# Conversion pieces moved into the expert slots, the first relu on ScalarE, the next tokens turned later

## The chip, the cores and the metric

One core of one Trainium2 chip runs the whole program. The metric is the device time of one execution in microseconds, as the median of several runs; a lower time is better.

## The reference

The program chains three layers on 1792 tokens of width 768. What matters here is the middle one, a layer of 8 experts, each token going to the one expert with the largest gate value:

```python
attn = 1.0 / (1.0 + np.exp(-scores));  x = attn @ v            # 4 x 12 heads, 448 x 64
e_idx = np.argmax(x @ w_gate, axis=1)
for e in range(8):                                             # w1[e]: 768 x 1024, w2[e]: 1024 x 768
    h = np.maximum(x[e_idx == e] @ w1[e], 0.0)
    out[e_idx == e] = gate_w * eom * (h @ w2[e])
h = out @ w_in;  return (h * np.cos(h)) @ w_out                # w_in: 768 x 2048, w_out: 2048 x 768
```

The weights `w_in` and `w_out` of the last layer arrive as 64-bit floats, the others as 32-bit floats.

## The kernel before

**Numbers.** A matrix product is made of three matmuls: each 32-bit operand is split into a high part (rounded by ScalarE, `hi`) and a low part (the rest, by VectorE, `lo`), and high x high, high x low and low x high are added up in PSUM. The helper `split` does this for raw expert weights (L217 on ScalarE, L218 on VectorE).

**Stages.** Attention takes the first 240 us or so, the experts go on to about 598 us, and the last layer follows.

**Slots.** After the tokens have been sorted by expert, the expert stage works in slots of 128 tokens: `slot(s, ...)` (L737) for s = 0, 1, 2 and so on. An expert has one slot or more; a slot either goes on with the expert of the slot before or begins a new one. Which slots are new, and which are used at all, is known only at run time: flags in `fl` are read into registers, and `tc.If(new != 0)` guards what a new expert needs. Slots 0 to 13 are always used (`NSURE` is 14), later ones are under a branch of their own. In this execution slots 0 to 18 are used, and 4, 6, 10, 11, 14, 15 and 18 begin an expert.

**One slot on TensorE.** The first product has two halves of 512 columns, each with 6 steps of 3 matmuls (`mm1`). Each half goes through a relu (`hr0`, `hr1`), is turned by 4 transposes and split (`turn_h`: `hh` on ScalarE, `hl` on VectorE). The second product has 8 steps of 6 matmuls (`mm2`), the first four of which use the first half. The next slot's tokens, gathered by GpSimd, are turned by 6 transposes and split into `xh` and `xl` (`turn`, L228). At the end `scale_y` scales the result, and SP stores it.

**The order.** The schedule is manual: every engine's queue holds its instructions in the order in which the program issues them. In a slot with s > 1 VectorE's order is: relu `hr0`; low part of the second weights 0 (`split2(0)`); `hl` of the first half; low part 1; relu `hr1`; `xl` (two operations); low parts 2 and 3; `hl` of the second half; the four low parts of the next expert's first weights (`split1(s + 1)`); the scaling; a conversion piece. ScalarE has the high parts at the same places. The low and high parts of weights are there only in slots that begin an expert, or stand before one.

**Weight loads.** The raw weights of an expert pass through four buffers `rw`. When `split1` has split a quarter of the first weights, SP loads a quarter of the second weights into the same buffer (L735); when `split2(i)` has split that, SP loads a quarter of the following expert's first weights (L757).

**Conversion pieces.** The 64-bit weights of the last layer are brought into high and low parts in 48 pieces. `conv(i)` is a generator with a first part (ScalarE two operations, GpSimd a maximum, VectorE two operations, L154 to L158) and, after a `yield`, a second part (VectorE four operations, L160 to L163). `conv_step` ends a begun piece, lets SP store the finished one and load the piece after this one, and begins the next; with `whole` it runs both parts at once. 23 pieces are converted during attention; before the change slots 1 to 17 do one whole piece each at their end, as the last lines of `slot` say, and the last 8 come in the last stage.

Of the kernel before, what the change touches and what calls it, by code (L numbers as in the profile page):

```python
# [22 lines left out]

GATE_STEPS = 7
NEST = 18
CONV_EARLY = 40
PAUSE = "pause"
NRING = 6
ROUTE_AT = [(0, "relu"), (0, 9), (0, 13), (0, 15), (1, 0), (1, 3), (1, "relu"), (1, 9), (1, 14)]
# [25 lines left out]
def tile_attn_moe_cos(ctx: ExitStack, tc: tile.TileContext, q, k, v, wg, wog, w1, w2, w_in, w_out, out):  # L55
# [13 lines left out]
    NSURE = -(-NT // P)  # L69
# [60 lines left out]
    def conv_load(i):  # L130
        if i >= len(conv_list):
            return
        which, h, r = conv_list[i]
        raw = craw[i % 2]
        if which == "i":
            src = w_in[r * P : (r + 1) * P, h * CW : (h + 1) * CW].bitcast(U32)
            nc.sync.dma_start(raw.rearrange("p f t -> p (f t)"), src)
        else:
            src = wo_in[h][:, :, r * CO : (r + 1) * CO].bitcast(U32)
            nc.sync.dma_start(raw.rearrange("p (two f) t -> p two (f t)", two=2), src)  # L140
# [25 lines left out]
    def conv_store():  # L166
        while conv_out:
            which, h, r, parts_ = conv_out.pop()
            for t, f in enumerate(parts_):
                if which == "i":  # L170
                    c0 = h * CW // P
                    nc.sync.dma_start(
                        wi_d[c0 : c0 + CW // P, :, t, r, :].rearrange("c p f -> p c f"),
                        f.rearrange("p (c f) -> p c f", f=P),
                    )
                else:
                    nc.sync.dma_start(
                        wo_to[h, t][:, :, r * CO : (r + 1) * CO], f.rearrange("p (two f) -> p two f", two=2)
                    )

    conv_at = [0]

    def conv_step(whole=True):
        conv_end()
        conv_store()
        conv_load(conv_at[0] + 1)
        conv_rest.append(conv(conv_at[0]))
        next(conv_rest[0], None)
        conv_at[0] += 1
        if whole:  # L190
            conv_end()
# [3 lines left out]
    def conv_end():  # L195
        while conv_rest:
            next(conv_rest.pop(), None)
# [9 lines left out]
    def w1_src_d(e, i):  # L207
        nh, kg = divmod(i, 2)
        return w1[bass.ds(e, 1)].rearrange("o (k p) f -> p (o k) f", p=P)[
            :, 3 * kg : 3 * kg + 3, 512 * nh : 512 * nh + 512  # L210
        ]
# [4 lines left out]
    def split(raw, hi, lo, pool):  # L216
        nc.scalar.activation(hi, raw, AF.Copy)  # L217
        (nc.gpsimd if pool else nc.vector).tensor_tensor(lo, raw, hi.bitcast(F32), op=ALU.subtract)  # L218

    def gather(xg, at, rows=NT):  # L220
        nc.gpsimd.indirect_dma_start(
            out=xg,
            out_offset=None,
            in_=x_d[:rows, :],
            in_offset=bass.IndirectOffsetOnAxis(ap=at, axis=0),
        )

    def turn(xg, ps, tag):  # L228
        for k0, n_ in ((0, 4), (4, 2)):
            pt = ps.tile([P, 512], F32, tag=tag, name="pxt")  # L230
            for kc in range(n_):
                nc.tensor.transpose(pt[:, kc * P : (kc + 1) * P], xg[:, (k0 + kc) * P : (k0 + kc + 1) * P], ident)
            ptv = pt[:, : n_ * P].rearrange("p (k t) -> p k t", t=P)
            nc.scalar.activation(xh[:, k0 : k0 + n_], ptv, AF.Copy)  # L234
            nc.vector.tensor_tensor(
                xl[:, k0 : k0 + n_], ptv, xh[:, k0 : k0 + n_].bitcast(F32), op=ALU.subtract
            )

    def mm1(ps, nh, kc, first, last):
        i = 2 * nh + kc // 3  # L240
        wh, wl = w1h[i][:, kc % 3, :], w1l[i][:, kc % 3, :]
        nc.tensor.matmul(ps, xh[:, kc], wh, start=first, stop=False)  # L242
        nc.tensor.matmul(ps, xh[:, kc], wl, start=False, stop=False)  # L243
        nc.tensor.matmul(ps, xl[:, kc], wh, start=False, stop=last)  # L244


    with ExitStack() as st:
# [314 lines left out]
        for i in range(n):  # L562
# [8 lines left out]
            elif 6 <= i < 6 + NSLOT - NSURE:  # L571
                s = NSURE + i - 6
# [109 lines left out]
    with ExitStack() as st:  # L682
        wp = st.enter_context(tc.tile_pool(name="wp", bufs=1, reuse_waits="tile"))
        m2 = st.enter_context(tc.tile_pool(name="m2", bufs=2, reuse_waits="tile"))
        ps_t = st.enter_context(tc.tile_pool(name="ps_t", bufs=4, reuse_waits="tile", space=PSUM))
# [6 lines left out]
        xgs = [xg0] + [wp.tile([P, DM], F32, name="xg1")]  # L692
        ysbs = [wp.tile([P, ROW], F32, name=f"ysb{i}") for i in range(3)]

        def relu(ps, scalar=False):
            hr = m2.tile([P, 512], F32, tag="hr", name="hr")
            if scalar:
                nc.scalar.activation(hr, ps, AF.Relu)
            else:
                nc.vector.tensor_scalar(hr, ps, 0.0, None, op0=ALU.max)  # L700
            return hr
# [22 lines left out]
        def flag(row, s, engines, top=1):  # L724
            return nc.values_load(fl[0:1, row, s : s + 1], engines=engines, min_val=0, max_val=top)
# [11 lines left out]
        def slot(s, between, when):  # L737
            nxt = s + 1 < NSLOT
            ahead = min(s, 1)
            hh = m2.tile([P, KF, P], F32R, tag="hh", name="hh", bufs=1)  # L740
            hl = m2.tile([P, KF, P], F32R, tag="hl", name="hl", bufs=1)
            with when():
                if 0 < s < NSLOT - 2:
                    gather(xgs[s % 2], idx[:, s + 2 : s + 3])
                if s > 1:
                    new = flag(1, s, SPLIT)
                    ld = flag(3, s, [ENG.SP])
                    ne = flag(0, s, [ENG.SP], E - 1)

                def split2(i):  # L750
                    if s == 0:
                        split(w2r[i], w2h[i], w2l[i], i in (0, 2))
                    elif s > 1:
                        with tc.If(new != 0):
                            split(w2r[i], w2h[i], w2l[i], False)
                        with tc.If(ld != 0):
                            nc.sync.dma_start(w1r[i], w1_src_d(ne, i))  # L757

                ph = p0 if s == 0 else ps_h.tile([P, 512], F32, tag="h", name="p0")
                for kc in range(3 if s == 0 else 0, KD):  # L760
                    mm1(ph, 0, kc, kc == 0, kc == KD - 1)
                    between(kc)
                hr0 = relu(ph)
                between("relu")
                split2(0)
                p1 = ps_h.tile([P, 512], F32, tag="h", name="p1")
                for kc in range(KD):
                    mm1(p1, 1, kc, kc == 0, kc == KD - 1)
                    if kc == 2:
                        turn_h(hr0, hh, hl, 0)  # L770
                        split2(1)
                    between(KD + kc)
                hr1 = relu(p1, s <= 1)
                if 0 < s and nxt:
                    turn(xgs[(s + 1) % 2], ps_t, "t")
                if s > 0:
                    split2(2)
                    split2(3)
                py = ps_y.tile([P, 2, 512], F32, tag="y", name="py")
                state["py"] = py  # L780
                for kc in range(ahead):
                    mm2(py, hh, hl, kc)
                    between(2 * KD + kc)
                turn_h(hr1, hh, hl, 1)
                between("h")
                if s == 0:
                    split2(2)
                    split2(3)
            if nxt and s >= NSURE:
                split1(s + 1)  # L790
            with when():
                for kc in range(ahead, KF):
                    mm2(py, hh, hl, kc)
                    between(2 * KD + kc)
                if s == 0:
                    turn(xgs[1], ps_t, "t")
                elif nxt and s < NSURE:
                    split1(s + 1)
                if s > 0:
                    scale_y(s)  # L800
            if s >= 1 and conv_at[0] < CONV_EARLY:
                conv_step()

        def scale_y(s):
# [7 lines left out]
        def store_y(s):  # L812
            nc.sync.dma_start(ys_d[s * P : (s + 1) * P, :], ysbs[s % 3])
# [191 lines left out]
        def between(s):  # L1005
            def step(k):
                for _ in range(ROUTE_AT.count((s, k))):
                    next(route, None)

            return step  # L1010
# [2 lines left out]
            split(w1r[i], w1h[i], w1l[i], pool)  # L1013
            nc.sync.dma_start(w2r[i], w2_src_d(e1[0], i))
        def last_slots(s):
            assert conv_at[0] >= CONV_EARLY
            act = nc.values_load(fl[0:1, 2, s : s + 1], min_val=0, max_val=1)
            with tc.If(act != 0):
                slot(s, between(s), nullcontext)
                store_y(s)  # L1020
                if s + 1 < NSLOT:
                    last_slots(s + 1)
# [22 lines left out]
    with ExitStack() as st:  # L1045
# [178 lines left out]
        for u in range(N):  # L1224
# [3 lines left out]
            turn = ()  # L1228
            if bi + 1 < len(blocks):
                if 1 <= c < 5:  # L1230
                    gather_y(bi + 1, c - 1)
                if 8 <= c < 8 + KD:
                    turn = turn_y(bi + 1, c - 8)
# [43 lines left out]
```

## Time and profile before

| | us |
|---|---|
| median of 3 runs | 1092.7 |
| lowest and highest of them | 1090.5, 1092.93 |
| the profiled execution: its time | 1094.78 |
| its span in the profile | 1093.0 |
| TensorE matmul busy in it | 1040.6 (95%) |
| VectorE busy | 703.8 (64%) |
| ScalarE busy | 486.1 (44%) |

The profile is of one execution. Its span runs from the first instruction to the last; the execution's own time is a little longer. PE is TensorE (PEld its weight loads), DVE is VectorE, ACT is ScalarE, POOL is GpSimd, SP issues most DMAs. Matmuls are pipelined, so that the recorded time of one is longer than the distance to the next. Times in the timeline count from the start of the span.

### The profile page before, as it was taken

The page shows a single profiled execution, that of the slowest core. Times are in us where ns is not written, and L with a number is a line of the kernel's source. Part 1 is how long each engine was busy: PE and PEld are TensorE (multiplying, and loading weights), DVE is VectorE, ACT ScalarE, POOL GpSimd, SP SyncE. Part 2 cuts the span into 40 slices and gives each one's busy share as a digit, 9 for nine tenths or more (in the row PEclk, how much of TensorE's full clock was granted, in tenths as well). Part 3 has the DMA queues.
Part 4 walks back from the last instruction along what each step waited for, and adds up shares of the span by engine and source line. Part 5 has one row for each costly group of instructions (what it writes and reads, how often), then busy time and mean ns, then how long its engine had stood idle before and what let it go on. Part 6 is the DMA issues. An engine that isn't in the chain of part 4 may idle for free. (4 is left out here: it accounts for less than half of the span.)

```text
span 1093.0 us, 16911 instructions
## 1 busy us (share of the span) xinstructions
PE 1040.6 (95%) x5836; PEld 832.6 (76%) x5836; DVE 703.8 (64%) x1229; ACT 486.1 (44%) x706; POOL 186.1 (17%) x189
## 2 busy tenths in 40 slices
PE   7999998889999999899798899999999999999997
PEld 4555555468878887687687788788888899999996
DVE  3778778576667458658747589865455555665553
ACT  6777775532435246336334344334323343334332
POOL 4433332521210211210211032103000020001001
PEclk9999999999999999899999999999999999999999
DMA  6999895635488429839845998656744478667741
GB/s 193 269 292 301 248 270 178 229 109 198 143 291 290 145 96 333 301 132 345 275 140 192 350 376 313 246 204 245 253 180 174 176 286 302 258 234 281 258 170 44
DMA packets 118788, 254.68 MB, mean 233 GB/s; under 512 B 9440, under 2 KB 66016, under 8 KB 118688
## 3 DMA queue, kind: packets, MB, share of 16 engines
q1 hardware_dynamic: 114768, 234.19, 63.1%
q0 software_dynamic: 3920, 19.28, 4.7%
q8 instruction: 48, 0.79, 0.3%
q14 instruction: 52, 0.43, 0.1%
HBM read 207.02 MB, written 46.41 MB: 232 GB/s over the span
## 5 line engine op out<-in xcount | busy, mean ns | idle before, releaser
L1169 PE MATMUL o<-wo,gh 128*128 128x512 f32 x448 | 168.4, 397 | 0.0
L155 POOL TENSOR_SCALAR cta<-cta 128x512 f32<-128x512 f32 x48 | 77.4, 1613 | 458.6 <-ACT cta L154 439.0
L1109 PE MATMUL ph<-yh,wi 128*128 128x512 f32 (+1 forms) x318 | 115.3, 363 | 0.2 <-DMA wi<-wi_d 0.2
L1110 PE MATMUL ph<-yl,wi 128*128 128x512 f32 (+1 forms) x318 | 115.2, 362 | 0.0
L1111 PE MATMUL ph<-yh,wi 128*128 128x512 f32 (+1 forms) x318 | 115.1, 362 | 0.0
L301 ACT ACTIVATE aT<-sc,b_sig 112x896 f32<-112x896 f32 x96 | 91.7, 1005 | 49.3 <-PE sc L298 48.1
L1132 ACT ACTIVATE r<-r 128x512 f32<-128x512 f32 (+1 forms) x64 | 37.0, 579 | 168.2 <-DVE r L1127 166.6
L1170 PE MATMUL or<-wo,gh 128*128 128x256 f32 x384 | 108.3, 282 | 0.0
L1169 PEld LDWEIGHTS o<-wo,gh 128*128 128x128 f32 x448 | 84.2, 188 | 17.0
L242 PE MATMUL p<-w1h,xh 128*128 128x512 f32 x228 | 93.2, 409 | 0.5 <-ACT xh L234 0.5
L243 PE MATMUL p<-w1l,xh 128*128 128x512 f32 x228 | 90.9, 398 | 0.5 <-DVE w1l L218 0.5
L244 PE MATMUL p<-w1h,xl 128*128 128x512 f32 x228 | 90.5, 397 | 0.0
L1169 PE MATMUL o<-wo,gl 128*128 128x512 f32 x224 | 88.2, 394 | 0.0
L305 PE MATMUL av<-aT,v 112*64 112x448 f32 x384 | 84.2, 561 | 0.0
L1138 DVE TENSOR_TENSOR r<-r,p 128x512 f32<-128x512 f32 (+1 forms) x64 | 40.0, 626 | 66.4 <-ACT r L1133 66.4
L1193 POOL DMA_INDIRECT out_dram<-osb,at x14 | 14.2, 1017 | 368.3 <-DVE osb L1182 277.0
L1170 PEld LDWEIGHTS or<-wo,gh 128*128 128x128 f32 x384 | 72.3, 188 | 0.8
L1123 DVE TENSOR_SCALAR t<-p 128x512 f32<-128x512 f32 (+1 forms) x64 | 27.2, 425 | 65.7 <-ACT p L1118 65.7
L709 ACT ACTIVATE hh<-pht 128x512 fp32r<-128x512 f32 x38 | 22.8, 599 | 101.4 <-PE pht L706 91.2
L1118 ACT ACTIVATE p<-ph 128x512 f32<-128x512 f32 (+1 forms) x64 | 34.7, 542 | 71.5 <-PE ph L1111 71.5
L1109 PEld LDWEIGHTS ph<-yh,wi 128*128 128x128 f32 x318 | 59.7, 188 | 8.4 <-DMA wi<-wi_d 0.7
L1143 DVE TENSOR_TENSOR gl<-r,gh 128x512 fp32r<-128x512 f32 (+1 forms) x64 | 42.5, 664 | 36.4 <-ACT gh L1142 36.4
(257 smaller groups left out, 2454.1 us busy)
## 6 DMA issues: line engine op xcount, KB each, us to landing
rw<-in_moe_w_dram SPq DMA_DIRECT2D x64, 768.0 KB, 6.5
wo<-wo_d SPq DMA_DIRECT2D x64, 768.0 KB, 4.5
wi<-wi_d SPq DMA_DIRECT2D x53, 768.0 KB, 6.0
craw<-in_moe_w_in_dram SPq DMA_DIRECT2D x25, 512.0 KB, 6.3
craw<-in_moe_w_out_dram SPq DMA_DIRECT2D x24, 512.0 KB, 5.3
er<-wi_d SPq DMA_DIRECT2D x11, 768.0 KB, 6.1
ys_d<-ysb SPq DMA_DIRECT2D x19, 384.5 KB, 3.6
wi_d<-chi SPq DMA_DIRECT2D x24, 256.0 KB, 3.8
```

Source lines behind the costliest of these rows:

```text
L155: nc.gpsimd.tensor_scalar(ta.bitcast(F32), ta.bitcast(F32), LEAST, None, op0=ALU.max)
L242: nc.tensor.matmul(ps, xh[:, kc], wh, start=first, stop=False)
L243: nc.tensor.matmul(ps, xh[:, kc], wl, start=False, stop=False)
L244: nc.tensor.matmul(ps, xl[:, kc], wh, start=False, stop=last)
L301: nc.scalar.activation(aT[:, c], ps[:, :, :S], AF.Sigmoid, bias=b_sig[:CP], scale=1.0 / math.sqrt(D))
L305: nc.tensor.matmul(pav[D * j : D * j + D, :S], t["v"][:, j, c, :], aT[:, c, j], start=c == 0, stop=c == NC - 1)
L1109: nc.tensor.matmul(ph[:, :w], wih[:, kc], yh[:, kc, :w], start=kc == 0, stop=False)
L1110: nc.tensor.matmul(ph[:, :w], wih[:, kc], yl[:, kc, :w], start=False, stop=False)
L1111: nc.tensor.matmul(ph[:, :w], wil[:, kc], yh[:, kc, :w], start=False, stop=kc == KD - 1)
L1143: nc.vector.tensor_tensor(gl[:, :w], r, gh[:, :w].bitcast(F32), op=ALU.subtract)
L1169: nc.tensor.matmul(acc[i], g[:, ts_], w[:, :512], start=f, stop=l)
L1170: nc.tensor.matmul(acc["r", i], g[:, ts_], w[:, 512:], start=f and (own or i % 2 == 0), stop=l, skip_group_check=True,)
```

## The change

- The first relu of a slot (`hr0`) runs on ScalarE instead of VectorE in all slots but slot 0.
- In those slots its transposes come after step 3 of the second half of the first product instead of step 2, and `split2(1)` moves from there behind the second relu.
- `split2(2)` and `split2(3)` come behind the transposes of the second half (`turn_h(hr1, ...)`) instead of ahead of them.
- In slots 1 to 13 the next tokens are turned after step 3 of the second product instead of before its first step; in the later slots they stay where they were, behind `split2(1)` now.
- The 17 conversion pieces of the slots no longer stand at the end of slots 1 to 17. Eight slots (`CONV_1ST`) begin a piece behind the turning of the first half, and end it (`conv_end`) behind the second weights' splits. Six of them (`CONV_2ND`) then begin a second piece, which ends behind the turning of the next tokens. Three slots (`CONV_END`) do a whole piece at their end. "Begin" includes the store of the piece before and the load of the next on SP.

```diff
-CONV_EARLY = 40
+CONV_1ST = (1, 2, 3, 6, 7, 8, 11, 12)
+CONV_2ND = (2, 3, 6, 7, 8, 11)
+CONV_END = (14, 15, 17)
...
-                hr0 = relu(ph)
+                hr0 = relu(ph, s > 0)
...
-                    if kc == 2:
+                    if kc == (3 if s > 0 else 2):
                         turn_h(hr0, hh, hl, 0)
-                        split2(1)
+                        if s == 0:
+                            split2(1)
+                        if s in CONV_1ST:
+                            conv_step(False)
                     between(KD + kc)
                 hr1 = relu(p1, s <= 1)
-                if 0 < s and nxt:
+                if s > 0:
+                    split2(1)
+                if s >= NSURE and nxt:
                     turn(xgs[(s + 1) % 2], ps_t, "t")
-                if s > 0:
-                    split2(2)
-                    split2(3)
...
                 turn_h(hr1, hh, hl, 1)
                 between("h")
-                if s == 0:
-                    split2(2)
-                    split2(3)
+                split2(2)
+                split2(3)
+                conv_end()
+                if s in CONV_2ND:
+                    conv_step(False)
...
                     mm2(py, hh, hl, kc)
                     between(2 * KD + kc)
+                    if kc == 3 and 0 < s < NSURE:
+                        turn(xgs[(s + 1) % 2], ps_t, "t")
+                        conv_end()
...
-            if s >= 1 and conv_at[0] < CONV_EARLY:
+            if s in CONV_END:
                 conv_step()
```

## Rows read from the trace of the kernel before

**Rows 1.** Busy time by slot: start:end, length, busy (count) by engine, clock, DMA.
```profile
277.83:296.05 18.22, 18.22 (x100) 15.46 (x99) 12.57 (x17) 9.48 (x11) 2.83 (x2) 1.00 0.42 135
...
334.51:354.41 19.90, 18.81 (x101) 15.39 (x99) 15.57 (x20) 9.29 (x11) 2.64 (x2) 1.00 1.01 351
354.41:372.75 18.34, 18.33 (x100) 15.45 (x99) 7.69 (x14) 3.88 (x7) 2.82 (x2) 1.00 0.41 133
...
409.39:429.31 19.92, 18.78 (x101) 15.39 (x99) 16.52 (x21) 11.31 (x13) 2.65 (x2) 1.00 1.01 344
429.31:456.83 27.52, 21.62 (x101) 17.48 (x99) 20.33 (x22) 13.21 (x14) 2.95 (x2) 0.88 0.90 312
...
493.27:514.42 21.15, 18.83 (x100) 15.41 (x99) 18.98 (x22) 12.34 (x14) 2.63 (x2) 1.00 0.99 345
514.42:540.28 25.86, 20.06 (x100) 16.57 (x99) 17.77 (x21) 12.04 (x13) 2.95 (x2) 0.93 0.94 315
540.28:559.02 18.74, 18.32 (x100) 15.46 (x99) 7.70 (x14) 3.87 (x7) 2.82 (x2) 1.00 0.70 212
...
577.53:598.20 20.67, 18.69 (x100) 15.27 (x98) 15.95 (x20) 9.29 (x11) 2.87 (x2) 1.00 0.63 219
```

**Rows 2.** Timeline of TensorE, slots 4, 11 and 15: start, length, instruction, [idle before].
```profile
307.74 0.66 PE L706 MATMUL pht<-ident,hr 128*128 128x128 f32 x4 [0.71 <-DVE hr L700]
...
441.05 0.47 PE L706 MATMUL pht<-ident,hr 128*128 128x128 f32 x1 [4.61 <-DVE hr L700]
...
525.71 0.69 PE L706 MATMUL pht<-ident,hr 128*128 128x128 f32 x2 [4.96 <-DVE hr L700]
```

**Rows 3.** Timeline of VectorE in slot 11, up to the first relu.
```profile
434.46 1.76 DVE L218 TENSOR_TENSOR w1l<-rw,w1h 128x1536 fp32r<-128x1536 f32 x1 [0.21 <-ACT w1h L217]
...
437.73 0.47 DVE L160 TENSOR_SCALAR cta<-cta 128x512 uint32<-128x512 uint32 x1
...
440.31 0.69 DVE L700 TENSOR_SCALAR hr<-p 128x512 f32<-128x512 f32 x1 [0.19 <-issue]
```

**Rows 4.** Busy time in slot 11 behind the long wait, columns as in rows 1.
```profile
441.05:445.80 4.75, 4.75 (x13) 3.78 (x14) 3.90 (x3) 1.97 (x2) 0.00 (x0) 0.50 1.04 394
```

**Rows 5.** Timeline of slot 3, all engines.
```profile
279.36 1.63 POOL L155 TENSOR_SCALAR cta<-cta 128x512 f32<-128x512 f32 x1 [15.22 <-ACT cta L154]
279.87 0.78 DVE L158 SCALAR_TENSOR_TENSOR ctu<-ctb,ctu 128x512 f32<-128x512 uint32 x1 [0.23 <-ACTq L754]
...
284.02 0.66 PE L706 MATMUL pht<-ident,hr 128*128 128x128 f32 x4
285.35 0.69 DVE L710 TENSOR_TENSOR hl<-pht,hh 128x512 fp32r<-128x512 f32 x1 [1.38 <-ACTq L754]
286.62 0.82 PE L232 MATMUL pxt<-ident,xg 128*128 128x128 f32 x6
288.32 0.60 PE L706 MATMUL pht<-ident,hr 128*128 128x128 f32 x4
289.55 1.49 ACT L217 ACTIVATE w1h<-rw 128x1536 fp32r<-128x1536 f32 x1
```

**Rows 6.** Groups by line, whole span: count | busy us, mean ns | idle before.
```profile
L217 ACT ACTIVATE w2h<-rw 128x1536 fp32r<-128x1536 f32 x32 | 46.6, 1484 | 5.1 <-DMA rw<-in_moe_w_dram 5.1
L154 ACT ACTIVATE cta<-craw 128x512 f32<-128x512 f32 x48 | 32.0, 668 | 3.3 <-DMA craw<-in_moe_w_in_dram 2.7 <-DMA craw<-in_moe_w_out_dram 0.4
L698 ACT ACTIVATE hr<-p 128x512 f32<-128x512 f32 x2 | 1.2, 598 | 1.5 <-PE p L244 1.4
```

**Rows 7.** DMA issues in slot 6: count, KB each, median us to landing.
```profile
rw<-in_moe_w_dram SPq DMA_DIRECT2D x5, 768.0 KB, 6.8
craw<-in_moe_w_in_dram SPq DMA_DIRECT2D x1, 512.0 KB, 9.8
```

**Rows 8.** Line 735, the loads of second weights.
```profile
DMA to landing us min/median/max: 4.2/6.5/9.1
```

More of the change, by code (lines that the diff above doesn't have):

```diff
@@ L1015, in last_slots @@
         def last_slots(s):
-            assert conv_at[0] >= CONV_EARLY
+            assert s > max(CONV_END)
             act = nc.values_load(fl[0:1, 2, s : s + 1], min_val=0, max_val=1)
```

## Prediction

> **What bounds the kernel now.** I first read the busy time slot by slot, a row for each of the 18 expert slots after the first [rows 1]. In a slot that goes on with an expert TensorE is busy nearly all the time: slots 3, 7 and 16 take 18.22, 18.34 and 18.74 us, and the seven more of their kind that are not shown lie between 18.21 and 18.51 (slot 1, with the routing in it, takes 19.62). A slot that begins an expert shows by its VectorE work (20 operations and more). There are seven: 4, 6, 10, 11, 14, 15 and 18 (4 takes 20.13, much as 10). They hold the idle TensorE time, and 11 and 15, which follow another new expert at once, hold most of it: 9.3 and 7.6 us above slot 3.
>
> Then I read who ended TensorE's waits, in the timeline [rows 2]. The long ones stand before the transposes of a relu's result: 4.61 us in slot 11, 4.96 in slot 15, and 0.71 before the second relu's in slot 4. VectorE's timeline shows why in slot 11 [rows 3]: the last low part of the first weights ends at 436.22, then come the scaling of the slot before and a whole conversion piece (its second half begins at 437.73), and the first relu only at 440.31. The relu is late because it stands in VectorE's order behind the piece. After that wait the granted clock is 0.50, the 1.2 GHz level, for 13 matmuls [rows 4]. The mean clock, 0.88 in slot 11 and 0.93 in slot 15, puts that loss at up to 0.12 x 27.52 = 3.3 and 0.07 x 25.86 = 1.8 us [rows 1].
>
> The change touches what lies between 240 and 598 us. Attention before it and the last stage behind it issue what they did: 23 pieces are converted ahead of the slots and 17 in them, as ever.
>
> **First relu on ScalarE.** It costs 0.60 there [rows 6], and ScalarE is busy 4 to 13 us of a slot [rows 1]. It waits for the product and for what ScalarE has to do before, so the waits of 4.6 and 5.0 go. In slot 15 a piece stays ahead (one of three still put at a slot's end): the scaling and the piece's two ScalarE operations, 0.67 each, leave some 0.6 of wait.
>
> **Pieces inside the slot.** In slots 1, 2, 3, 6, 7, 8, 11 and 12 a piece's first part now stands behind the first half's low part and ahead of the second relu on VectorE (in slot 1 that relu is on ScalarE). Worked from slot 3 [rows 5], in us after its start at 277.83: the transposes of the first relu, at 6.19, come three matmuls later, at 6.9 (27 took the 6.19). Its high part ends 1.33 later, when the low part can begin: 8.2. The piece's first ScalarE operation, 0.67, ends at 8.9; GpSimd's maximum starts then, and VectorE's second operation of the piece ends 1.29 after that start (279.36 to 280.65): 10.2. The relu, 0.69, ends at 10.9. TensorE would be there at 10.49 (288.32) less the six token transposes that moved away, 0.82 with their tail and some 0.7 without: 9.8. So it waits 1.1 in each such slot. The bounds: nothing, if the piece is through before the product is, and 2.2, if the relu also had to wait for most of the maximum. I take 1.1, since each step of it is a row. Slots 2 and 3: +1.1 each, slot 8 +1.0, slot 1 +0.3: **+3.5**.
>
> On this chain the Trainium skill has a rule that speaks against the change (SBUF — State Buffer, section "SBUF: two separate sides"): VectorE with two SBUF inputs and GpSimd reading SBUF lock one pair of ports against each other, and the loser waits for the whole instruction. The trace does not agree: in slot 3 VectorE's operation with two SBUF inputs ran from 279.87 to 280.65, inside the maximum's 279.36 to 280.99 [rows 5]. The sum by that rule is among the rivals; it goes by the row here.
>
> **Second parts and second pieces.** The second half of a piece, 2.4 us of VectorE (437.73 to 440.12 [rows 3]), moves behind the last low parts, where about 7 us of TensorE work follow; that work hides it, and without it the next tokens would be 2.4 late. Slots 2, 3, 6, 7, 8 and 11 start a second piece before the next tokens are turned, and of these 6 and 11 begin an expert. There the second piece's load is issued on SP behind the reload of the first raw weights, which waits for the first low part of the second weights, 8.2 into the slot (relu over at 4.95, then 1.49 [rows 6] and 1.76 [rows 3]); with the two stores before it, it goes out at about 9.5. Even with SP free such a load landed 9.8 after its issue in slot 6, behind weights that took 6.8 [rows 7]. So it lands 19 us into a slot of 19.2. ScalarE's two operations (1.2, overlapped) stand ahead of the next tokens' high part (0.6) and VectorE's ahead of their low part (0.7): with the gaps 2.65 after the landing, 21.7, where TensorE wants it at 19.7. Slot 7 starts 2.0 late, slot 12 by the same count 2.1, and each waits 1.1 for its own piece: 21.3 against 18.34, and 21.4 against 18.2: **+6.2**. Landings of 18 and 19.7 would give 1.0 and 2.7, and behind the weights of slot 11, itself late, up to 5.4 in slot 12: the term lies between +3 and +10.
>
> **New experts.** The next tokens are turned after four steps of the second product, at 13.3 to 14.0. Their high parts end at 14.9, and only then ScalarE splits the next first weights, which it began at 11.7 before (289.55, [rows 5]): some 3.1 later. The first low part is ready at 18.1, just as the slot ends, and the load behind it starts then. In slot 4 a second piece of slot 3 stands before it on VectorE, a wait of 1.8 at the start, which eats the slot's gain (0). Elsewhere the load lands 4.2 after issue [rows 8] and the relu is over at 4.95; with 1.49, 1.76 and the half's low part of 0.69 that is 8.9, wanted by the second product at 9.3: no wait. The second relu no longer stands behind a low part of 1.76, nor the last low part behind two of them, so waits like the 0.71 go. Slot 10: 18.2, -1.7. Slots 14 and 18 keep the token turn ahead, 0.6: 18.8 and 18.7, -2.3 and -2.0. Slot 6 waits 1.1 for its piece: 19.2, -0.7. **-6.7**; bounds -3 (other waits turn up behind those removed) and -8 (none is left).
>
> Slot 11: 18.2, plus 1.5 for the first low part (its loads come at the pace of the DMA, share 1.01 in slot 10), 0.4 for the second weights, 1.6 for the second relu behind low part and piece: 21.7, -5.8. No wait comes near the 4.6 ahead of the half clock, so I count none of that. Slot 15: 18.2 + 0.7 (first low part) + 0.6 (relu) + 2.5 (second weights' low part behind a whole piece on VectorE) + 1.5 (their third low part behind the tokens'): 23.5, -2.4. **-8.2**; bounds -11 and 0, the latter if the landing of the weights sets the pace at each step.
>
> **Slots with no piece before or in them** (5, 9, 13, 16, 17; in 16 it no longer matters) fall to 18.2: **-1.3**, between -1.5 and 0.
>
> **Sum:** 3.5 + 6.2 - 6.7 - 8.2 - 1.3 = -6.5 us. The profiled execution took 1094.78, 1.78 more than its span of 1093.0, and lies 2.1 above the median of 1092.7; against its own time that is 1088.3, against the median **1086.2**.
>
> **Rivals.**
> *Pieces free.* Neither the second relu nor the next tokens wait for a piece: +3.5 and +6.2 go, -16.2 is left, 1076.5. For it: VectorE and ScalarE are far from full in slot 3 [rows 1]. Against: their order is fixed, and the chain above is of recorded steps.
> *Late second pieces.* Their loads land at the upper bound, +10 for +6.2: -2.7, 1090.0, no change by the line below. For it: DMA share 1.01 in slots 6 and 10 [rows 1]. Against: the landing of 9.8 was behind stores and a gather too.
> *Port lock.* VectorE's second operation of the piece starts only at the end of GpSimd's maximum, 280.99 for 279.87, in seven slots: +7.7, so +1.2, 1093.9. Against it: they ran together [rows 5]. This is what the Trainium skill's SBUF — State Buffer says in "SBUF: two separate sides".
> *Late weights, the slower side.* The second weights are asked for 3.1 us later. If their first load lands L after its issue, TensorE waits L - 5.4 (9.3 less 1.49, 1.76 and 0.69) before the second product in slots 4, 6, 10 and 14. The longest landing is 9.1 [rows 8]: 4 x 3.7 = 14.8, so +8.3, 1101. It decides from L = 7.0 on and passes 0.3% slower at 7.9. For it: the median is 6.5. Against: the short landings come when the queue was empty, as it is at the starts of these slots.
>
> **How the numbers follow.** Forecast 0.58, pieces free 0.12, late second pieces 0.16, port lock 0.05, late weights 0.09. 0.3% (3.3 us) is about what a measurement can tell from no change: faster is below 1089.4, slower above 1096. The forecast and pieces free are faster but for 0.04 near the line; of late second pieces 0.02 are faster; port lock is no change; of late weights 0.08 are slower, and 0.03 more of the second pieces, should they meet other upper bounds. That gives 0.68, 0.21 and 0.11. The range 1080 to 1094 holds the forecast with its bounds, late second pieces and port lock, and leaves out most of pieces free and of late weights.
>
> **What would show it.** Right: no wait before the first relu's transposes; clock 1.00 in slot 11; waits near 1.1 before the second relu's in slots 2, 3, 7 and 8; slots 7 and 12 starting 2 us late behind the token turn; slot 11 below 23. Wrong: waits before the second product in slots 6, 10 and 14; a half clock in slot 11 or 15; slots 2 and 8 still at 18.2.

## The result, and the profile after

The changed kernel takes 1106.67 us (median of 4 runs, 1104.88 to 1108.48); the kernel before, run beside it, 1092.82. The ratio is 1.0114, with a 95% interval of 1.0087 to 1.014: slower, where 1086.2 and faster was predicted (range 1080 to 1094). The profiled execution took 1105.22, its span is 1103.5 against 1093.0, and 9.5 of these 10.4 us lie in slots 1 to 18.

The waits of TensorE between 240 and 600 us, grouped by what ended them (us in total, times, longest). First the main group of the kernel before:

```profile
PE pht L706 <- DVE hr L700: 15.5, 10, 5.0
```

and the groups after:

```profile
PE p L246 <- DVEq L736: 8.4, 5, 2.9
PE pht L709 <- DVEq L757: 4.9, 5, 1.0
PE p L246 <- DVE w1l L221: 4.8, 4, 2.4
PE py L722 <- DVE w2l L221: 3.5, 3, 2.7
PE p L245 <- ACTq L736: 2.7, 2, 1.3
PE pht L709 <- DVE hr L703: 2.3, 2, 1.2
```

The waits before the transposes of a relu (L706, now L709) shrank from 15.5 to 7.2, and all that is left of them stands before the second relu's. The long ones of [rows 2] are gone, as predicted. New is the start of a slot: the first matmul of the first product (L245, which needs `w1h`) and the second (L246, which needs `w1l`). The profile ends their waits with a queue, "ACTq" and "DVEq", that passes line 736. That line is `tc.If(new != 0)` in `split1`, the guard of the weight split, and not an operation on data.

Busy time by slot after (columns as in [rows 1]; a slot is taken from its first matmul at L245 to the next slot's), slots 3, 6, 7, 10, 11, 12, 14, 15, 16 and 18:

```profile
279.78:300.27 20.49, 18.59 (x101) 15.53 (x99) 10.55 (x21) 7.89 (x12) 4.51 (x3) 1.00 0.47 144
340.76:361.76 21.00, 18.47 (x101) 15.45 (x99) 18.90 (x22) 13.58 (x16) 3.28 (x3) 1.00 0.95 335
361.76:385.84 24.08, 20.30 (x98) 16.77 (x99) 12.49 (x24) 5.72 (x10) 5.50 (x4) 0.93 0.58 193
425.63:443.82 18.19, 18.19 (x100) 15.61 (x99) 15.73 (x15) 12.74 (x14) 2.53 (x1) 1.00 0.92 316
443.82:468.00 24.18, 19.54 (x101) 15.31 (x99) 20.31 (x22) 15.37 (x17) 3.78 (x3) 1.00 1.00 351
468.00:492.16 24.16, 20.30 (x99) 16.77 (x100) 10.18 (x19) 4.48 (x8) 7.55 (x7) 0.93 0.62 228
510.25:528.98 18.73, 18.35 (x100) 15.55 (x99) 16.82 (x16) 13.63 (x14) 0.00 (x0) 1.00 0.90 314
528.98:552.98 24.00, 20.69 (x101) 16.78 (x100) 18.84 (x21) 12.98 (x15) 2.95 (x2) 0.93 0.97 332
552.98:571.08 18.10, 18.10 (x101) 15.55 (x100) 7.00 (x13) 4.47 (x8) 3.77 (x3) 1.00 0.80 255
589.18:608.42 19.24, 18.50 (x100) 15.37 (x98) 16.20 (x19) 10.12 (x13) 3.81 (x2) 1.00 0.63 228
```

Slots 10 (18.2) and 14 (18.7) came out as predicted to 0.1, 16 too, 18 within 0.6. Slots 7 and 12, in which no expert begins, take 24.1 and 24.2 where 21.3 and 21.4 were predicted, and both now have a mean clock of 0.93; slot 11, at 0.88 before [rows 1], is at 1.00, and slot 15 stays at 0.93. Slot 4, not among these rows, is at 0.92 now and was at 1.00 before.

The start of slot 7 tells the story, in the timeline of VectorE, ScalarE and TensorE:

```profile
357.87 0.42 DVE L163 TENSOR_SCALAR cta<-cta 128x512 uint32<-128x512 uint32 x1
358.32 0.69 DVE L164 SCALAR_TENSOR_TENSOR chi<-craw,cta 128x512 uint32<-128x512 uint32 x1
...
359.05 0.68 ACT L157 ACTIVATE cta<-craw 128x512 f32<-128x512 f32 x1 [3.19 <-DVE chi L164]
...
360.81 0.85 ACT L237 ACTIVATE xh<-pxt 128x512 fp32r<-128x512 f32 x2
361.67 1.02 DVE L238 TENSOR_TENSOR xl<-pxt,xh 128x512 fp32r<-128x512 f32 x2
361.76 0.49 PE L245 MATMUL p<-w1h,xh 128*128 128x512 f32 x1 [1.33 <-ACTq L736]
362.60 0.42 DVE L163 TENSOR_SCALAR cta<-cta 128x512 uint32<-128x512 uint32 x1
...
364.23 0.69 DVE L166 TENSOR_TENSOR clo<-ctu,ctb 128x512 fp32r<-128x512 f32 x1
365.04 0.50 PE L246 MATMUL p<-w1l,xh 128*128 128x512 f32 x1 [2.79 <-DVEq L736]
...
365.98 0.63 PE L246 MATMUL p<-w1l,xh 128*128 128x512 f32 x1
```

No weights are split here (slot 7 goes on with an expert), yet the second matmul starts just when VectorE has ended the second piece's second part (`cta` 362.60 to `clo` 364.92) and passes the guard behind it. The first matmul's wait is another matter: `xh` ended at 361.66 and ScalarE passed its guard at once, 0.1 before the matmul. There the tokens are late, and not the guard. What holds the piece, and with it `xh`, are two things that end close together. The load was issued at 351.53 and landed 7.1 later (the group of DMA issues from 351 to 354; the load of [rows 7] took 9.8):

```profile
craw<-in_moe_w_in_dram SPq DMA_DIRECT2D x1, 512.0 KB, 7.1
```

That is 358.6. ScalarE's `abs` starts at 359.05, when VectorE's `chi` of the first piece has ended (359.01), since the two pieces share one buffer `cta`; the next tokens' `xh` stood behind it on ScalarE. So the buffer came 0.4 later than the load. In slot 11 the second piece waited for its load:

```profile
465.36 0.67 ACT L157 ACTIVATE cta<-craw 128x512 f32<-128x512 f32 x1 [3.26 <-DMA craw<-in_moe_w_out_dram]
```

Then the clock, in two stretches of slot 7 (length, TensorE busy, clock, DMA):

```profile
365.98:369.25 3.27, 3.27 (x9) 0.53 0.75 297
369.25:375.00 5.75, 5.75 (x29) 1.00 0.63 185
```

After 3.28 us with one matmul in them TensorE runs at about the 1.2 GHz level until 369.25 (0.63 us for a matmul that takes 0.39 otherwise). Slot 7 is 20.30 us busy; with the same work at clock 1.00 it is 18.69 (experiment 1), so this costs 1.6. Slot 4 shows the same behind one wait alone, for the low part of new weights:

```profile
303.09 0.50 PE L246 MATMUL p<-w1l,xh 128*128 128x512 f32 x1 [2.43 <-DVE w1l L221]
...
304.46 0.63 PE L245 MATMUL p<-w1h,xh 128*128 128x512 f32 x1
```

### The profile page after: what moved, and what is told of

Same layout as the page of the kernel before. It is cut to its first block, busy times and chain, and to the rows that moved or that the text cites. A ratio compares the mean times of both kernels' runs of the same rounds, so it can differ in the third digit from the quotient of the medians.

```text
span 1103.5 us, 17184 instructions
## 1 busy us (share of the span) xinstructions
PE 1044.6 (95%) x5836; PEld 837.0 (76%) x5836; DVE 693.3 (63%) x1211; ACT 497.0 (45%) x724; POOL 188.6 (17%) x189
## 5 line engine op out<-in xcount | busy, mean ns | idle before, releaser
L246 PE MATMUL p<-w1l,xh 128*128 128x512 f32 x228 | 92.8, 407 | 13.2 <-DVEq L736 8.4
L245 PE MATMUL p<-w1h,xh 128*128 128x512 f32 x228 | 94.0, 412 | 3.1 <-ACTq L736 2.7
L713 DVE TENSOR_TENSOR hl<-pht,hh 128x512 fp32r<-128x512 f32 x38 | 26.2, 689 | 79.7 <-ACTq L757 41.6
```

## The experiments

All times are medians; "before" ran beside each (1092.9 to 1094.3 us). Differences between two kernels are those of their medians, which come from different groups of runs; by the ratios to "before" the gain on the changed kernel is 11.7 for 13.7 in experiment 1 and 6.2 for 6.7 in experiment 3. The slots' lengths, of one execution each, are in a table at the end.

**1. Guard first.** The weight split, with its guard, goes ahead of the second piece's second part:

```
                         turn(xgs[(s + 1) % 2], ps_t, "t")
-                        conv_end()
...
                     split1(s + 1)
+                    conv_end()
```

> Only the order of two steps in slots 2, 3, 6, 7, 8 and 11 is turned: the weight split with its guard stands ahead of the second piece's second part, whose first part stays where it was. Guard theory: the five waits of TensorE for VectorE's guard (0.9, 2.8, 0.8, 1.0 and 2.9, in sum 8.4) go, the wait for ScalarE's guard (1.3, twice) stays, since ScalarE's part of the piece still stands ahead of it: about 1098 (1095 to 1101). Late-landing and port-lock theories: nothing changes in the loads or in who works beside whom, 1105 to 1108.

1092.97 (ratio to before 1.0007, 0.9983 to 1.003): 13.7 less than the changed kernel. The guard theory holds and the others fall, though the gain is larger than its 8.4 us of waits and the time lies below its range. The same place in its timeline:

```profile
357.61 1.01 DVE L238 TENSOR_TENSOR xl<-pxt,xh 128x512 fp32r<-128x512 f32 x2
357.70 0.49 PE L245 MATMUL p<-w1h,xh 128*128 128x512 f32 x1 [1.33 <-ACTq L736]
358.74 0.50 PE L246 MATMUL p<-w1l,xh 128*128 128x512 f32 x1 [0.54 <-DVE xl L238]
359.69 0.43 DVE L163 TENSOR_SCALAR cta<-cta 128x512 uint32<-128x512 uint32 x1 [1.06 <-DVEq L736]
```

TensorE waits 0.54 for `xl` in place of 2.79, and the piece's second part follows. The rest of the gain: slot 7 is at clock 1.00 again (row below: 18.69 busy for 20.30), slots 4 and 12 too, and in slot 4 the low part of the new weights no longer stands behind the piece (its wait is 0.68 for 2.43, the slot 20.09 for 22.41).

```profile
357.70:377.93 20.23, 18.69 (x99) 1.00 0.69 233
```

**2. Second pieces at the slots' ends.** `CONV_2ND` is empty, `CONV_END` is (2, 3, 6, 7, 8, 11, 14, 15, 17).

> The six second pieces leave the inside of slots 2, 3, 6, 7, 8 and 11 and stand whole at the ends of the same slots, behind the guarded weight split and the scaling, as pieces stood in the kernel before; first pieces stay. Guard theory (the next slot's first matmuls wait until VectorE has passed the weight split's guard, which stands behind the second piece): the waits at the start of slots 3, 4, 7, 8, 9 and 12 go, slots 7 and 12 come back from 24.1 to about 19.3, the time is about 1092 (1089 to 1096). Late-landing theory (the loads of the second pieces arrive late): the loads now have a whole slot, about 1100. Port-lock theory (VectorE slowed while GpSimd works): the number of pieces is the same, no change, 1105 to 1107.

1102.6 (1.0077; 1.0054 to 1.0101): only 4 less than the changed kernel, so my number missed by 10. Slots 3, 8 and 9 behaved (19.9, 19.3, 18.1), but slot 7 took 25.0 and slot 12 28.1. The timeline of slot 12 says why:

```profile
466.87 0.35 SPq L140 DMA_DIRECT2D craw<-in_moe_w_in_dram  x1
475.38 0.43 DVE L160 TENSOR_SCALAR ctb<-craw 128x512 uint32<-128x512 uint32 x1 [5.02 <-SPq L736]
477.24 0.68 DVE L703 TENSOR_SCALAR hr<-p 128x512 f32<-128x512 f32 x1
477.98 1.11 PE L709 MATMUL pht<-ident,hr 128*128 128x128 f32 x4 [6.61 <-DVEq L757]
```

The whole piece at the end of slot 11 runs in the first microseconds of slot 12; only then SP issues the load of slot 12's own piece (466.87). VectorE takes it up at 475.38, 8.5 us later, and the second relu stands behind it: 6.6 us of wait on TensorE. So the late-landing theory is real here, for a first piece that follows a whole one closely. In the changed kernel two of the six second pieces waited for their load (3.20 in slot 2, 3.26 in slot 11), the other four for `chi`; the waits for VectorE's guard stood in slots behind either kind.

**3. First piece behind the second relu.** The lines `if s in CONV_1ST: conv_step(False)` move from the turn of `hr0` to right after `hr1 = relu(p1, s <= 1)`.

> The eight first pieces begin one step later: VectorE takes the second relu before the first part of the piece. Theory that the wait before the second relu's transposes (0.93 to 1.20 in slots 2, 3, 6, 7, 8, 11, 12) is that order alone: these waits go, about 7 less, 1099.5 (1097 to 1103); the waits at the next slots' starts stay. Rival (the piece only moves its cost on, since second pieces then begin later and VectorE reaches the guard later still): 1104 to 1109.

1099.93 (1.0057; 1.0038 to 1.0077): 6.7 less than the changed kernel, as expected. Slot 2 goes from 19.44 to 18.54, and no wait for the second relu is left; the waits at the slots' starts stay.

**4. No piece inside.** `CONV_1ST` and `CONV_2ND` are empty, `CONV_END` is 1 to 17: of the change only the relu and the order of steps stay.

> No piece inside a slot: 17 whole pieces at the ends of slots 1 to 17 as in the kernel before; of the change only the first relu on ScalarE, the later turn of the next tokens and the order of the split stay. Guard theory: nothing stands ahead of the guard, slots 2 to 9 and 12 go back to about 18.3, while slots 10, 14, 15, 16 to 18 keep their gain: 1082 to 1088. Rival (the new order of turn and split is what costs): 1093 or more. Rival (the slots with a new expert were cheaper only because they had no piece at their end): 1089 to 1093.

1091.44 (0.9983; 0.9962 to 1.0004): the last rival's number, not mine. Slots 2, 3, 5, 7 to 9 are at 18.1, but 4, 6, 10 and 14 are longer than in the kernel before (21.9, 22.1, 21.8, 22.2). The main group of waits, and slot 10's timeline:

```profile
PE py L722 <- DVE w2l L221: 13.9, 7, 3.1
```

```profile
418.43 0.42 DVE L160 TENSOR_SCALAR ctb<-craw 128x512 uint32<-128x512 uint32 x1
...
422.27 1.76 DVE L221 TENSOR_TENSOR w2l<-rw,w2h 128x1536 fp32r<-128x1536 f32 x1 [0.32 <-issue]
424.08 0.66 PE L722 MATMUL py<-w2l,hh 128*128 128x512 f32 x1 [1.78 <-DVE w2l L221]
```

The first weights are split later by the new order: their low parts end 4.9 us into slot 10, against 1.8 with the relu alone (experiment 5). The piece from the end of slot 9 comes behind them (418.43 on), and behind it the first low part of the second weights starts only at 422.27, when TensorE wants it (at 422.30). With this order the gain of the new-expert slots hangs on there being no piece at the end of the slot before.

**5. The relu alone.** The kernel before with `hr0 = relu(ph, s > 0)`.

> The kernel before with one part of the change alone: the first relu on ScalarE in every slot but the first. The prediction's theory (TensorE's 15.5 us of waits for VectorE's relu are saved where the relu leaves VectorE): 1086 to 1089. Rival, from the run with all pieces at the slots' ends (its slots 4, 6, 10 and 14 wait for the split second weights instead, 13.9 us in all): the wait only moves on to the next product of VectorE or ScalarE, 1091 to 1095.

1087.93 (0.9952; 0.9933 to 0.9971): faster by 5, as expected; in slot 11 2.2 is saved, in 14 1.4, in 18 1.1. Slot 15 saves nothing (26.1 for 25.9): the relu's wait of 4.96 went, but one of 2.65 for the second weights came, and the mean clock is 0.87. Next to experiment 4 it says that the new order costs about 3.5 where whole pieces stand at all slots' ends; the two intervals overlap a little.

**6. Maximum on VectorE.** In `conv`, `(nc.vector if 23 <= i < 40 else nc.gpsimd)` does the maximum.

> The changed kernel with the maximum of the 17 pieces in slots on VectorE instead of GpSimd, so that GpSimd computes nothing beside VectorE in these slots. Port-lock theory (GpSimd's maximum slows or stops VectorE's two-input work beside it): the slowed 0.78 to 0.90 us go back to 0.69, TensorE's waits shrink, 1095 to 1103. Guard theory: VectorE gets some 0.4 to 0.7 us more per piece ahead of the guard and of the second relu, the waits grow, 1106 to 1112.

1111.53 (1.0166; 1.0134 to 1.0198): slower by 4.9 than the changed kernel, as the guard theory said, and not faster, as the lock would have it. VectorE now has the maximum to do as well, so the time alone does not measure the lock. What GpSimd does to VectorE can be read from the groups by line (count | busy, mean ns); first the changed kernel, then this one:

```profile
L161 DVE SCALAR_TENSOR_TENSOR ctu<-ctb,ctu 128x512 f32<-128x512 uint32 x17 | 13.1, 772 | 2.3 <-ACT ctu L159 0.7
```

```profile
L161 DVE SCALAR_TENSOR_TENSOR ctu<-ctb,ctu 128x512 f32<-128x512 uint32 x17 | 11.8, 692 | 1.8
```

**7. Guard first, and the first piece behind the second relu** (experiments 1 and 3 together, the piece also behind `split2(1)`).

> The two edits together that were tried alone: the guarded weight split ahead of the second piece's second part, and the first piece begun behind the second relu (here behind the split of the second weights too). If the two waits are separate costs, the gains add: 13.7 + 6.7 off 1106.7, 1086 (1083 to 1090). If the later first piece makes the second one late (its load is issued only 3 us ahead of its use), ScalarE holds the next tokens' xh behind it and slots 3, 4, 7, 8, 9, 12 get longer: 1090 to 1096.

1096.02 (1.0027; 1.0007 to 1.0047): the gains do not add. The waits before the second relu's transposes are gone, but slots 6, 7, 11, 12 and 15 are longer than in experiment 1 (22.66 for 20.98 in slot 6; slot 15 is not touched by the edit). Timeline at the end of slot 6:

```profile
347.89 0.75 SPq L140 DMA_DIRECT2D craw<-in_moe_w_in_dram  x1
355.05 0.66 ACT L157 ACTIVATE cta<-craw 128x512 f32<-128x512 f32 x1 [6.42 <-DMA craw<-in_moe_w_in_dram]
357.12 0.49 PE L245 MATMUL p<-w1h,xh 128*128 128x512 f32 x1 [2.97 <-ACTq L736]
```

Here the second piece does wait for its load, 6.4 us, as the rival said, and holds `xh` and ScalarE's guard behind it.

**8. Guard first, second piece behind the token turn.** `conv_step(False)` for `CONV_2ND` moves from the second relu's turn to just behind `turn(xgs[...])` in the second product.

> As the kernel with the guard first, and the second piece is begun behind the next tokens' turn, not ahead of it, so that ScalarE's abs, which waits 2.4 to 3.2 us for the first piece's second part (one buffer for both), no longer stands ahead of xh. Theory: TensorE's waits for ScalarE's guard and for xh and xl at the slots' starts (2.7 + 0.5 + 1.1) go, 1093 - 4 = 1089 (1087 to 1091). Rival (the piece then holds ScalarE's and VectorE's guards instead, behind the abs and the copy): 1092 to 1096.

1092.43 (0.9996; 0.998 to 1.0012): the rival. The waits for `xh` and ScalarE's guard halve (2.7 to 1.4), but VectorE's guard is late again, 2.9 in two waits, now behind the piece's first part; slot 7 takes 22.89.

**9 and 10. Pieces re-placed, with both orders.** From the table of experiment 4 I read where a piece costs nothing: at the end of a slot whose follower begins no expert, and from the second relu's turn on in a slot that goes on with one, if its second part stands behind guard and scaling. The places fit the routing of tokens in these data.

```
-CONV_1ST = (1, 2, 3, 6, 7, 8, 11, 12)
-CONV_2ND = (2, 3, 6, 7, 8, 11)
-CONV_END = (14, 15, 17)
+CONV_1ST = ()
+CONV_2ND = (1, 2, 3, 7, 8, 12, 16)
+CONV_END = (1, 2, 4, 6, 7, 8, 11, 12, 15, 16)
...
-                        conv_end()
...
                     scale_y(s)
+                conv_end()
```

> The changed kernel's relu and order of steps, with the 17 pieces put only where neither the slot's own weights nor the next slot's are split beside them: seven begin at the second relu's transposes in slots 1, 2, 3, 7, 8, 12 and 16 and end behind the guard and the scaling, ten stand whole at the ends of slots 1, 2, 4, 6, 7, 8, 11, 12, 15 and 16, thus in the first part of the next slot. Theory that a piece costs only where it stands ahead of a guard, a split or a relu that TensorE waits for: slots 2, 3, 5, 7 to 9, 12, 13, 16, 17 at 18.1, 4, 6 and 10 at 18.1 to 18.5, 14 at 18.7, 18 at 19.2, 11 and 15 at 22 to 24: 1075 (1072 to 1080). Rival (17 pieces cost the slots a certain time wherever they stand, VectorE's or GpSimd's work in itself): 1086 or more.

> The same places of the pieces with the order of steps of the kernel before (second weights split and tokens turned as before) and the first relu on ScalarE. If the order of the change is worth something by itself once no piece stands near the new experts: slots 4, 6, 10 stay near 19.6 as in the kernel with the relu alone, 1080 to 1084. If the places of the pieces were all: the same time as the run beside it, within 2.

With the order of the change 1080.07 (0.9874; 0.9849 to 0.99), with the order of before 1087.12 (0.9919; 0.9896 to 0.9943). The order is worth 7 us by the medians, 4.9 by the ratios, once no piece stands ahead of a new expert (slots 6 and 10: 18.55 and 18.39 for 19.67 and 19.65), where it cost about 3.5 with pieces at all ends. My 1075, and the 1080 to 1084 of the second, missed because of slot 2, 23 us in both. Timeline of the first kernel there:

```profile
263.34 0.36 SPq L140 DMA_DIRECT2D craw<-in_moe_w_in_dram  x1
269.01 0.68 ACT L157 ACTIVATE cta<-craw 128x512 f32<-128x512 f32 x1 [7.53 <-DMA craw<-in_moe_w_in_dram]
270.78 1.11 PE L709 MATMUL pht<-ident,hr 128*128 128x128 f32 x4 [3.21 <-ACTq L757]
```

It is experiment 2 again, on ScalarE: the whole piece at the end of slot 1 waits for a load that SP issues 2.8 us into slot 2, when it has gone through the routing's weight loads and two stores that slot 1's own piece put ahead of it; the first relu stands behind that piece.

**11. The piece inside slot 1 moved to slot 13.** `CONV_2ND = (2, 3, 7, 8, 12, 13, 16)`.

> As the first of the two kernels with pieces re-placed, but the piece that begins inside slot 1 goes to slot 13. Theory: slot 2 lost 4.8 there because the whole piece at the end of slot 1 stood on ScalarE ahead of the first relu and waited 7.5 us for a load that could only be issued behind slot 1's own piece; with one piece in slot 1 that load is in time, slot 2 is 18.1, slot 13 and 14 grow by 1 at most: 1075.5 (1073 to 1078). Rival (whichever piece opens slot 2 is late, since the routing's loads stand ahead): slot 2 stays near 23, 1080.

1074.35 (0.9834; 0.9807 to 0.986), the best: slot 2 at 18.1, slot 14 longer by 1.3. The main group of its waits in the slots, and busy time in slots 11 and 15:

```profile
PE p L246 <- DVE w1l L221: 3.0, 4, 1.1
```

```profile
423.17:444.39 21.22, 19.22 (x100) 15.34 (x99) 16.14 (x15) 12.64 (x13) 0.00 (x0) 1.00 0.99 323
...
500.58:521.54 20.96, 19.30 (x100) 15.39 (x99) 16.52 (x15) 13.06 (x13) 0.00 (x0) 1.00 0.94 315
```

All 17 pieces are still done between 240 and 600 us, and every slot from 2 on that goes on with an expert is at 18.1: well placed, they cost next to nothing. Slots 11 and 15, now with no piece ahead of them or in them but one at their own ends, keep 21, at a DMA share of 0.99 and 0.94 and at clock 1.00.

## Why the prediction was wrong

The terms of the sum, each as predicted and as measured: the lengths of its slots in a profiled execution, less those of before, added up. The middle columns are the changed kernel and experiment 1, the last is experiment 11.

| Term (slots) | Predicted | Changed kernel | Guard first | Best |
|---|---|---|---|---|
| Pieces inside (1, 2, 3, 8) | +3.5 | +5.7 | +3.5 | +0.6 |
| Second parts and pieces (7, 12) | +6.2 | +11.7 | +3.9 | -0.4 |
| New experts (4, 6, 10, 14, 18) | -6.7 | -2.3 | -4.7 | -7.8 |
| Slots 11 and 15 | -8.2 | -5.2 | -4.9 | -11.2 |
| No piece near (5, 9, 13, 16, 17) | -1.3 | -0.4 | -1.7 | -1.7 |
| Sum | -6.5 | +9.5 | -3.9 | -20.5 |

**The step that failed** is the first sentence of "Second parts and second pieces": that a piece's second half "moves behind the last low parts, where about 7 us of TensorE work follow; that work hides it". For a first piece it does. For a second piece the second half stands at the slot's end, ahead of the guard of the next slot's weights on VectorE. I asked only what the next tokens wait for, and charged that order in slot 4 alone, where weights are split; in slots 3, 7, 8, 9 and 12, where none are, it stood at nothing. There the second matmul waits until VectorE has passed line 736, though no branch is taken: 8.4 us in five slots. The half clock that follows was put at nothing too, for the reason that no wait would come near 4.6; it came behind waits of 2.43 to 2.86, in slots 4, 7, 12 and 15. Experiment 1 moves that order alone and takes 13.4 of the 16.0 us between the predicted and the measured sum: VectorE's guard waits go, slot 4's wait shrinks by 1.75, and slots 4, 7 and 12 are at full clock again. With it the first term is the predicted +3.5.

**Pieces inside the slot.** Right, but for the guard. The waits before the second relu's transposes are 0.93 to 1.20 for the 1.1 worked out, and experiment 3 takes them away for 6.7. Slots 3 and 8 have 0.9 and 0.8 of guard wait on top. Slot 6 was to be 19.2 with the same 1.1; it took 21.0 even in experiment 1: with slots taken from their first matmul, 1.33 of it is the wait for `xh` that the prediction charged to slot 7.

**Second parts and second pieces.** The late tokens came nearly as worked out; what was missing is the guard. In experiment 1 the first two matmuls wait 1.33 and 0.54 in slot 7, 1.32 and 0.55 in slot 12, 1.9 for the 2.0 and 2.1 of the prediction. The table counts the 1.3 in slots 6 and 11; counted as the prediction does, the term is 3.9 + 2.65 = 6.5 there, for +6.2. The cause was half right: in slot 6 the load landed 18 us into the slot, for the 19 worked out, but the shared buffer `cta`, which the prediction left out, came free 0.4 later, and in experiment 1 slot 11's piece too waited for `chi`. By these times either alone would have held slot 6's piece to within 0.4 of where it was; that was not tried apart. That late loads can cost more, experiments 2, 7 and 9 show, in other places.

**New experts.** Slots 10, 14 and 18 came within 0.6. Slot 4 was to gain nothing, and lost 2.3: its first low part stood behind the piece of slot 3, as foreseen, but the wait was 2.43 (at 303.09) for 1.8, and the half clock followed it. The "no wait" ahead of the second product held: none of more than 0.4 in slots 4, 6, 10 and 14, so the rival of late weights did not occur, though its time, 1101, is the nearest of all.

**Slots 11 and 15.** The relu's wait of 4.6 and 5.0 went; the half clock with it in slot 11. But 3.0 of the expected 8.2 did not come; 1.3 of that is the wait for `xh` at the end of slot 11. Experiment 11 shows that 3 us above 18.1 stay in each with no piece ahead of them, so these are not the pieces' doing. Slot 15 has one wait of 2.66 before the second product, which I had at 2.5, and a clock of 0.93 that I had not counted: the half clock named as a sign of being wrong. Its length is no fine measure: in experiments 1, 2, 3, 7 and 8, whose edits touch neither it nor slot 14, it lies between 24.1 and 26.6.

**Port lock.** The durations in experiment 6 settle it: VectorE's operation takes 772 ns on average beside GpSimd's maximum (six of the 17 take 0.90 us, ten the 0.69 that they take without) and 692 without. So it is slowed by 0.08, in sum 1.4 us for 17 pieces, and nowhere stopped for a maximum of 1.5 to 2.8. The rule of the Trainium skill (SBUF — State Buffer, section "SBUF: two separate sides") that the loser waits for the whole instruction is not what this pair of operations showed.

**Open.** What the clock alone cost was not tried apart from the waits ahead of it, nor load and buffer apart from each other; and what sets the 3 us that are left in slots 11 and 15 (DMA share 0.94 and more) is not known.

Slots' lengths in the profiled executions, us:

| Slot | Before | Changed | 1 guard first | 2 | 3 | 4 | 5 relu | 7 | 8 | 9 | 11 best |
|---|---|---|---|---|---|---|---|---|---|---|---|
| 2 | 18.2 | 19.4 | 19.4 | 19.4 | 18.5 | 18.1 | 18.1 | 18.5 | 19.4 | 23.0 | 18.1 |
| 3 | 18.2 | 20.5 | 19.3 | 19.9 | 19.6 | 18.1 | 18.1 | 18.1 | 19.3 | 18.1 | 18.1 |
| 4 | 20.1 | 22.4 | 20.1 | 21.9 | 24.0 | 21.9 | 19.7 | 20.1 | 20.1 | 19.1 | 19.1 |
| 6 | 19.9 | 21.0 | 21.0 | 20.0 | 20.3 | 22.1 | 19.7 | 22.7 | 20.8 | 18.6 | 18.1 |
| 7 | 18.4 | 24.1 | 20.2 | 25.0 | 23.6 | 18.1 | 18.1 | 20.7 | 22.9 | 18.1 | 18.1 |
| 10 | 19.9 | 18.2 | 18.1 | 18.1 | 18.1 | 21.8 | 19.7 | 18.1 | 18.1 | 18.4 | 18.1 |
| 11 | 27.5 | 24.2 | 24.4 | 22.6 | 24.0 | 23.9 | 25.4 | 26.5 | 23.2 | 21.7 | 21.2 |
| 12 | 18.2 | 24.2 | 20.2 | 28.1 | 22.7 | 19.8 | 18.1 | 21.2 | 21.0 | 18.3 | 18.1 |
| 14 | 21.2 | 18.7 | 18.8 | 18.7 | 18.7 | 22.2 | 19.7 | 18.7 | 18.8 | 18.7 | 20.0 |
| 15 | 25.9 | 24.0 | 24.1 | 25.3 | 25.0 | 23.9 | 26.1 | 25.2 | 26.6 | 20.8 | 21.0 |

## What to carry to other kernels

Work that is "hidden" must be followed to everything behind it on its own engine, a guard that is not taken included: another engine may wait for that queue to pass it, though no instruction under it runs. So put optional work behind such a guard, and the loads for it at least one landing (here 4 to 10 us) ahead of the engine that meets them in order. And measure the parts of a change together with where the rest stands: the same order of steps cost about 3.5 us with pieces at every slot's end and gave 5 to 7 with the pieces elsewhere.

## What was not expected of the hardware

A not-taken branch on VectorE's queue ended waits of TensorE of 0.8 to 2.9 us, five times in one execution; the same branch on ScalarE's queue, which the profile names for 1.33 twice, came at once behind `xh`, whose end lies 0.1 before the matmul. And TensorE, which lost its 2.4 GHz level behind the long waits of slots 11 and 15 before, lost it behind shorter ones too: in slot 7 after 1.33 and 2.79 with a single matmul between them (0.63 us a matmul up to 369.25, about 1.6 us in all, more than half the price of the longer wait itself), in slot 4 after one wait of 2.43.
